# Attention and two feed-forward layers on one core: loading order and bias rows of the first heads

## The chip, the cores and the metric

The kernel runs on one core of a Trainium2 chip. The metric is the device time of one execution in microseconds, the median of the runs shown. All the work of the program, from the first load of its inputs to the last store of its output, lies in that time. TensorE is called PE below, VectorE DVE, ScalarE ACT, GpSimd POOL and SyncE SP, as the profile names them; SP issues nearly all DMAs, in order, on one queue.

## What is computed

The reference has three stages. The first is causal attention over 4 batches of 8 heads, 576 positions and a head dimension of 64, with a bias that comes from a running sum over the positions:

```
scores = scale * q @ k.T
cum    = cumsum(max(s, 0))                      # s: one number per position
scores = where(causal, -1e9, scores + min(-(cum[i] - cum[j]), 0))
attn   = softmax(scores);  x = attn @ v         # heads side by side: 2304 x 512
h = x @ w_in;  g = softplus(h);  x = g @ w_out                  # d_ff 2048
h = x @ w2_in; g = P(h) / (Q(h) + 1e-6);  out = g @ w2_out      # cubic over quadratic
```

The weights of both feed-forward layers arrive as 64-bit words, which the kernel turns into two 32-bit parts (high and low) on DVE, ACT and POOL.

## The kernel before

The kernel is recorded in an order of its own and then planned: `Planner` (L187) takes every recorded instruction as a `Step` with a modelled length (L109), walks through them engine by engine, and returns one order for each engine, which is kept up to a modelled time `UNTIL` (L70). A transfer's modelled length is its bytes over `DMA_RATE` plus `DMA_LATENCY` (L71). `queue_behind` (L445) ties newly recorded instructions behind the last one of their engine, so that the planner cannot put them in front of it. What has no such tie and no missing operand may be put anywhere.

Attention begins with "first" parts: the first 256 positions of the 16 heads of batches 0 and 1, handled as 8 pairs of heads. For pair i, `load_pair` (L507) loads q and k of two heads, 64 rows of 1024 numbers, into a tile `raw2` of 66 used rows. Rows 64 and 65 of that tile carry the running sum, so that one matmul of 66 rows gives score and bias together (L619). These two rows are called bias rows here. For pair 0 they are made in place: `load_s00` loads the two rows of s (tile `s00`), and `make_cum0` (L458) runs a scaling, a scan over both heads' 512 numbers and two scaled copies, one on ACT (L464) and one on DVE (L465). A zero in the tile `one` (L470) restarts the scan at the second head. For the other pairs the same is done once, on 16 rows for all eight pairs (`load_s0`, tile `s0_t`), into the tile `cumc`, and `load_cum` (L512) sends each pair's two rows from `cumc` to `raw2` by DMA.

`keep_order` (L437) fixes each engine's order in that preamble as it is written:

```
load_s00(); load_pair(0); load_s0()
for i in range(1, 4): load_pair(i)
load_v0(); make_cums()
for i in range(1, 4): load_cum(i)
```

Each head then goes through scores on PE (L619), masking with a row minimum (DVE, L595), exp (ACT, L612), the reciprocal of the sum (DVE, L613 and L614), a scaling (POOL, L615), three transposes (PE, L694), an evacuation (ACT, L673) and two matmuls with v (PE, L788). Tile `v2` holds v of four pairs. The results are split into high and low parts and feed the first layer (L1093 to L1095, then L1129 to L1131). Weight words come through `load_w` (L886) into tiles `raw64` and are turned in `conv_t` (L901; L908 to L910) and `conv_hl` (L913). The low parts are also stored to DRAM (L924) and read back as `w1l` (L934). The small vector `ab` of the second layer's coefficients is loaded into the tile `prm` and prepared by L1573 to L1576, which are recorded in the first layer.

At most eight transfers of SP are open at a time: transfer n waits until transfer n-8 has landed.

Of the kernel before, what the change touches and what calls it, by code (L numbers as in the profile page):

```python
# [8 lines left out]
F32 = mybir.dt.float32  # L9
F32R = mybir.dt.float32r  # L10
I32 = mybir.dt.int32
AF = mybir.ActivationFunctionType
# [55 lines left out]
          ("wide", "two"): 0.2, ("wide", "one"): 0.05, ("thin", "two"): 0.6, ("thin", "one"): 0.3}  # L68
HOLD, ROUNDS = 0.0, 6
UNTIL = 936.0  # L70
DMA_RATE, DMA_LATENCY, LANES = 320e3, 1.9, 8  # L71


class Access:
# [34 lines left out]
class Step:  # L109


    def __init__(self, i, tied):
        self.i, self.tied = i, tied
        self.engine = str(i.engine).split(".")[-1]
        acc = [[Access(x) for x in xs if getattr(getattr(x, "bass_ap", None), "tensor", None) is not None]
               for xs in (i.outs, i.ins)]
        self.outs, self.ins = acc
        self.dma, self.port = 0, None
        n = self.outs[0].elements if self.outs else 1
        psum = any(x.psum for x in self.outs + self.ins)  # L120
        wide = len(self.ins) > 1 and self.ins[1].dims[1][1] > 1
        if "DMA" in i.opcode:
            self.dma = 4 * n * self.outs[0].dims[0][1]
            self.busy = self.done = ISSUE.get(self.engine, 0.5)
        elif self.engine == "PE":
            turn = self.ins[0].tile.startswith("ident")
            full = not turn and "32r" not in str(i.ins[0].bass_ap.dtype)
            self.busy = 0.00085 * n if turn else 0.024 + 0.00162 * n if full else 0.012 + 0.000428 * n
            self.done = self.busy + 0.165
        elif self.engine == "Activation":  # L130
            more = max(0, len(self.outs) + len(self.ins) - 2)
            near = any(x.psum for x in self.ins)
            self.busy = (0.12 + 0.00079 * n + 0.07 * more) if near else (0.165 + 0.0008 * n + 0.095 * more)
            self.done = self.busy + 0.08
        elif self.engine == "DVE" and n == 1:
            self.busy, self.done = 0.115, 0.155
        elif self.engine == "DVE":
            one = len(self.ins) < 2 and not psum and i.opcode != "TensorCopy"
            self.busy = 0.06 + 0.00064 * n if one else 0.107 + 0.00105 * n
            self.done = self.busy + 0.06  # L140
            self.port = None if psum else "one" if one else "two"
        elif self.engine == "Pool":
            self.busy = 0.22 + 0.00205 * n if wide else 0.28 + 0.0007 * n
            self.done = self.busy + 0.03
# [42 lines left out]
class Planner:  # L187
# [27 lines left out]
    def forward(self, rank):  # L215
# [34 lines left out]
        for _ in range(n):  # L250
            best = None
            for e in self.engines:
                can = [(max(t, clock[e]), rank[k], k) for k in wait[e] for t in (earliest(k),) if t is not None]
                if can:
                    t0 = min(can)[0]
                    pick = min((c for c in can if c[0] <= t0 + HOLD), key=lambda c: (c[1], c[0], c[2]))
                    if best is None or pick[0] < best[0]:
                        best = pick
            t, _, k = best
            s = steps[k]  # L260
            wait[s.engine].remove(k)
            for x in tiles[k]:
                if x not in held:
                    tag = pool[x][0]
                    slots[tag].sort(key=lambda q: q[0])
                    self.slot_of[x] = slots[tag].pop(0)[1]
                    held.add(x)
                    last[tag] = max(last[tag], t)
                    while head[tag] < len(queue[tag]) and queue[tag][head[tag]] in held:
                        head[tag] += 1  # L270
            busy, done = s.busy, s.done
            if s.port:
                other = "Pool" if s.engine == "DVE" else "DVE"
                slow = SHARED.get((s.port, port[other]), 0.0) * max(0.0, min(clock[other] - t, busy))
                busy, done = busy + slow, done + slow
            port[s.engine] = s.port
            self.start[k], clock[s.engine] = t, t + busy
            self.end[k] = t + busy
            if s.dma:
                dma = max(dma, clock[s.engine]) + s.dma / DMA_RATE  # L280
                self.after[k] = dma + DMA_LATENCY - self.end[k]
                landed.append(dma + DMA_LATENCY)
            else:
                self.after[k] = done - busy
            done = self.end[k] + self.after[k]
# [54 lines left out]
def moe_chain_kernel(ctx, tc, qk0, v0, qk, vv, s0, s, w1, w2, ab, out):  # L340
    nc = tc.nc
# [9 lines left out]
    def t_w(name, shape, dt):  # L351
        return sb.tile(shape, dt, tag="W", bufs=NF, name=name)
# [99 lines left out]
        nc.sync.dma_start(out=cum_t["s00"][64:66], in_=s0[0:2])  # L452

    def load_s0():
        cum_t["s0"] = sb.tile([16, 2 * M + 4], F32, tag="tmp", bufs=1, name="s0_t")
        nc.sync.dma_start(out=cum_t["s0"], in_=s0)

    def make_cum0(st, one, t, to):  # L458
        n = 2 * M
        cst = st[:, n:n + 4]  # L460
        nc.vector.tensor_scalar(st[:, 0:n], st[:, 0:n], 0.0, 8.0, op0=ALU.max, op1=ALU.mult)
        nc.vector.tensor_tensor_scan(t, one, st[:, 0:n], 0.0, op0=ALU.mult, op1=ALU.add)
        t = t.rearrange("p (j s) -> p j s", j=2)
        nc.scalar.activation(to[:, :, 0], t, AF.Identity, scale=cst[:, 0:1], bias=cst[:, 1:2])  # L464
        nc.vector.tensor_scalar(to[:, :, 1], t, cst[:, 2:3], cst[:, 3:4], op0=ALU.mult, op1=ALU.add)  # L465

    def make_cums():
        one = t_w("one", [128, 2 * M], F32)
        nc.vector.memset(one, 1.0)
        nc.vector.memset(one[:, M:M + 1], 0.0)  # L470
        t = t_w("cum0", [128, 2 * M], F32)
        make_cum0(cum_t["s00"][64:66], one[64:66], t[64:66], raw2[0][64:66])
        cum_t["c"] = t_w("cumc", [16, 2, 2, M], F32)
        make_cum0(cum_t["s0"], one[0:16], t[0:16], cum_t["c"])

    def load_s():
        st = t_w("s_t", [128, S + 6], F32)
# [28 lines left out]

    def load_pair(i):  # L507
        t = t_q("raw2", [128, 2, 2, M], F32)
        nc.sync.dma_start(out=t[0:64], in_=qk0[i])
        raw2[i] = t  # L510

    def load_cum(i):  # L512
        nc.sync.dma_start(out=raw2[i][64:66], in_=cum_t["c"][2 * i:2 * i + 2])

    def load_v0():
        load_v2(0)
# [365 lines left out]
    xs_t = {}  # L882
    h_t, g_t, acc_t = {}, {}, {}
    raw64 = {}

    def load_w(m, ff, half, al=None):  # L886
        n = c2.index((ff, half)) if m else 0
        if n % 2:
            if "x" not in raw64:
                raw64["x"] = t_x("raw64x", [128, 2, 512, 2], I32)  # L890
            r = raw64["x"][:, n // 2 % 2]
        else:
            r = (al or t_r)("raw64", [128, 512, 2], I32)
        src = (w1, w2)[m][ff, :, half * 512:(half + 1) * 512].bitcast(I32)
        nc.sync.dma_start(out=r.rearrange("p a b -> p (a b)"), in_=src)
        raw64[m, ff, half] = r

    def conv(m, ff, half, hi, lo):
# [502 lines left out]
    if True:  # L1401
# [1 line left out]
        load_s00()  # L1403
        load_pair(0)
        load_s0()
        for i in range(1, 4):
            load_pair(i)
        load_v0()
        make_cums()
        for i in range(1, 4):  # L1410
            load_cum(i)
        order = keep_order()
        make_identity(nc, ident)
        nc.gpsimd.memset(mask, 0.0)
# [105 lines left out]
        for i in range(NU):  # L1520
# [41 lines left out]
            if u is not None:  # L1562
# [7 lines left out]
                if t4 >= 34 and t4 % 2 == 0 and FS + (t4 - 34) // 2 < NF:  # L1570
                    reload2(FS + (t4 - 34) // 2)
                if ph == 0 and T == 3 and ff == 8:
                    nc.sync.dma_start(out=abt, in_=ab)  # L1573
                    nc.vector.memset(qc, QC)
                    nc.vector.tensor_scalar(nega, abt[:, 0:4], -1.0, None, op0=ALU.mult)
                    nc.scalar.activation(babs, abt[:, 4:6], AF.Abs)  # L1576
                if ph == 0 and T == 5 and ff == 8:
                    load_y(0)
                if ph == 1:
# [102 lines left out]
```

## Time and profile before

| | us |
|---|---|
| median of 3 runs (lowest, highest) | 1022.59 (1021.87, 1023.67) |
| the profiled execution | 1024.62 |
| its span, first to last instruction | 1022.7 |
| PE busy | 998.6 (98%) |
| DVE busy | 789.9 (77%) |
| ACT busy | 763.7 (75%) |
| POOL busy | 469.1 (46%) |

Times in the profile count from the span's start. A row of the timeline is a run of like instructions on one engine; in brackets stands how long the engine was idle before it and what ended that. A wait is put down to the one that came last by the profile. A plain 32-bit matmul is counted as two instructions on PE, so that x4 in a row of L619 is the scores of one head. PEclk is the clock that the throttle granted to PE, as a share of full speed; a matmul's own duration tells beside it at which of its two levels (1.2 and 2.4 GHz) the array ran.

### The profile page before, as it was taken

The numbers are of one execution on the slowest core, as the hardware profiler recorded it, in microseconds if no ns is written. First come the engines' busy times: TensorE is split into PE (matmuls) and PEld (weight loads), VectorE is DVE, ScalarE is ACT, GpSimd is POOL, SyncE is SP. The second block draws the span as 40 slices with busy tenths as digits, with TensorE's granted clock in tenths as the row PEclk, the third lists the DMA queues.
The fourth block names the chain that finished last, engine by engine and source line by source line (L and its number), as shares of the span: only waits on it lengthen the run. The fifth ranks groups of instructions, "written<-read, shape, count | busy, mean of one in ns | idle before, by whom it ended". The sixth has DMA issues, their size and how long they took to land.

```text
span 1022.7 us, 18157 instructions
## 1 busy us (share of the span) xinstructions
PE 998.6 (98%) x5924; PEld 904.1 (88%) x5924; DVE 789.9 (77%) x1783; ACT 763.7 (75%) x1556; POOL 469.1 (46%) x464
## 2 busy tenths in 40 slices
PE   6989999999999999999999999999999999999998
PEld 5789999988999888899999999888888898889897
DVE  5799887877886887887677658887788778777765
ACT  5998777776885776776566667788779878788775
POOL 2776664411221112221446665676466457555542
PEclk9999999999999999999999999999999999999999
DMA  9778565474554654335999998628456656655300
GB/s 254 294 235 289 188 207 182 157 225 150 166 173 149 198 161 125 116 108 175 357 350 328 303 334 295 207 83 285 158 165 196 213 168 195 209 161 168 124 1 31
DMA packets 101069, 201.62 MB, mean 197 GB/s; under 512 B 11248, under 2 KB 30512, under 8 KB 100976
## 3 DMA queue, kind: packets, MB, share of 16 engines
q1 hardware_dynamic: 98432, 196.31, 58.6%
q10 hardware_dynamic: 2544, 4.16, 1.6%
q8 instruction: 47, 0.77, 0.3%
q14 instruction: 46, 0.38, 0.1%
HBM read 161.16 MB, written 35.19 MB: 192 GB/s over the span
## 4 chain that ended last, share of the span: by engine, by line
PE 87%; DVE 4%; DMA 3%; ACT 2%; POOL 2%; issue 1%; SPq 0%; POOLq 0%; DVEq 0%; ACTq 0%
PE h L1094 6%; PE at L1340 6%; PE h L1093 6%; PE h L1095 6%; PE at L763 5%; PE acc L1131 5%; PE acc L1130 5%; PE acc L1129 5%; PE h L1340 5%; PE acc L1270 4%; PE acc L1269 4%; PE acc L1271 4%; PE at L622 2%; PE at L623 2%; PE acc L1136 2%; PE acc L1137 2%
## 5 line engine op out<-in xcount | busy, mean ns | idle before, releaser
L615 POOL TENSOR_SCALAR PA<-PA,stat 128x384 f32<-128x384 f32 (+3 forms) x112 | 69.9, 629 | 179.7 <-DVE stat L614 113.4
L1093 PE MATMUL h<-xs,w1h 128*128 128x448 f32 (+1 forms) x360 | 122.9, 342 | 0.8 <-DVE stat L613 0.7
L1095 PE MATMUL h<-xs,w1l 128*128 128x448 f32 (+1 forms) x360 | 122.6, 342 | 0.9 <-DMA w1l<-l_d 0.8
L1094 PE MATMUL h<-xs,w1h 128*128 128x448 f32 (+1 forms) x360 | 122.6, 341 | 0.0
L1130 PE MATMUL acc<-gl,w1h 128*128 128x448 f32 (+1 forms) x352 | 119.3, 340 | 0.8 <-POOL gl L1397 0.8
L1131 PE MATMUL acc<-gh,w1l 128*128 128x448 f32 (+1 forms) x352 | 118.3, 339 | 0.3 <-POOL w1l L915 0.2
L1129 PE MATMUL acc<-gh,w1h 128*128 128x448 f32 (+1 forms) x352 | 118.4, 338 | 0.0
L1255 POOL TENSOR_TENSOR gl<-PA,gh 128x512 fp32r<-128x512 f32 x48 | 63.2, 1319 | 68.0 <-issue 51.7
L612 ACT ACTIVATE PA<-PA,stat 128x384 f32<-128x384 f32 (+3 forms) x112 | 63.9, 572 | 21.6 <-DVE stat L595 20.4
L1269 PE MATMUL acc<-w2b,gh 128*128 128x512 f32 x192 | 76.0, 396 | 0.0
L1270 PE MATMUL acc<-w2b,gh 128*128 128x512 f32 x192 | 75.8, 395 | 0.0
L1271 PE MATMUL acc<-w2b,gl 128*128 128x512 f32 x192 | 73.5, 394 | 0.0
L1093 PEld LDWEIGHTS h<-xs,w1h 128*128 128x128 f32 x360 | 68.0, 189 | 4.6 <-ACT pt L673 0.9
L1095 PEld LDWEIGHTS h<-xs,w1l 128*128 128x128 f32 x360 | 67.7, 188 | 4.8 <-DMA w1l<-l_d 1.0
L1094 PEld LDWEIGHTS h<-xs,w1h 128*128 128x128 f32 x360 | 67.9, 188 | 3.3
L1191 ACT ACTIVATE e<-h 128x448 f32<-128x448 f32 (+1 forms) x90 | 43.5, 483 | 36.2 <-PE h L1095 34.4
L1130 PEld LDWEIGHTS acc<-gl,w1h 128*128 128x128 f32 x352 | 66.2, 188 | 4.2 <-POOL gl L1397 1.0
L1131 PEld LDWEIGHTS acc<-gh,w1l 128*128 128x128 f32 x352 | 66.1, 188 | 3.6 <-POOL w1l L915 0.4
L1129 PEld LDWEIGHTS acc<-gh,w1h 128*128 128x128 f32 x352 | 66.2, 189 | 3.2
L1397 POOL TENSOR_TENSOR gl<-e,gh 128x256 fp32r<-128x256 f32 (+1 forms) x48 | 48.0, 1002 | 29.9 <-ACT gh L1395 21.0
L595 DVE CUSTOM_DVE_ANT_0 PA<-at,mask 128x384 f32<-128x384 f32 (+3 forms) x100 | 50.2, 519 | 7.4 <-PE at L623 5.0
L622 PE MATMUL at<-ht 128*128 128x512 f32 (+3 forms) x156 | 53.3, 347 | 0.1
(352 smaller groups left out, 3141.9 us busy)
## 6 DMA issues: line engine op xcount, KB each, us to landing
wa<-wa_d SPq DMA_DIRECT2D x100, 512.0 KB
w1l<-l_d SPq DMA_DIRECT2D x138, 256.0 KB
raw<-in_w_dram SPq DMA_DIRECT2D x48, 512.0 KB
raw<-in_qk_dram SPq DMA_DIRECT2D x24, 384.0 KB
l_d<-w1l SPq DMA_DIRECT2D x32, 256.0 KB
raw64x<-in_w_dram SPq DMA_DIRECT2D x16, 512.0 KB
wa_d<-pt SPq DMA_DIRECT2D x16, 512.0 KB
raw<-in_qk_dram SPq DMA_DIRECT2D x8, 576.0 KB
```

The lines of the kernel that those rows point to most:

```text
L615: nc.gpsimd.tensor_scalar(pt[:, 0:n], pt[:, 0:n], stat[:, i, 2:3], 1.0, op0=ALU.mult, op1=ALU.mult)
L622: nc.tensor.matmul(o, hq, p.ht[:, 1, k0:k0 + n], start=True, stop=False)
L1093: nc.tensor.matmul(h, wh[:, cs], xh, start=(k == 0), stop=False)
L1094: nc.tensor.matmul(h, wh[:, cs], xl, start=False, stop=False)
L1095: nc.tensor.matmul(h, wl[:, cs], xh, start=False, stop=(k == KD - 1))
L1129: nc.tensor.matmul(o, wh[:, cs], gh, start=first and not both, stop=False)
L1130: nc.tensor.matmul(o, wh[:, cs], gl, start=False, stop=False)
L1131: nc.tensor.matmul(o, wl[:, cs], gh, start=False, stop=last and (not both or m % 2 == 1))
L1269: nc.tensor.matmul(acc[m], gh[:, cs], wh, start=first, stop=False)
L1270: nc.tensor.matmul(acc[m], gh[:, cs], wl, start=False, stop=False)
L1271: nc.tensor.matmul(acc[m], gl[:, cs], wh, start=False, stop=last)
L1340: nc.tensor.matmul(o[:, p * 256:p * 256 + 256], x, z[:, k], start=first and p == k == n == 0, stop=(k, n) == (1, 2), skip_group_check=True)
```

## The change

The preamble is written in another order, and some tiles are laid out differently.

- Pair 0 is loaded in two transfers, one for each head (64 x 512 numbers each), and its bias rows are made head by head: a scaling, a scan and two copies of 256 numbers for head 0, then the same for head 1.
- The other pairs' bias rows are scanned with the heads on rows of their own: 48 rows of 256 numbers (rows 0 to 15 the first heads, 32 to 47 the second) in place of 16 rows of 512. The restart at column 256 falls away.
- v of batch 0 is loaded in two halves (pairs 0 and 1, pairs 2 and 3). The order on SP becomes pairs 0 and 1, half of v, pair 2, the bias rows of pairs 1 and 2, pair 3 and its rows, the rest of v.
- Each `load_w` is tied behind the one before it on SP, and the load of `ab` with its three small operations is tied behind what was recorded last on their engines.
- The planner's model changes: 400e3 in place of 320e3 for the transfer rate, twice the time for transfers of at most 64 rows, a length of its own for scans, and transfers that ACT issues no longer take SP's turn.

```
-DMA_RATE, DMA_LATENCY, LANES = 320e3, 1.9, 8
+DMA_RATE, DMA_LATENCY, LANES = 400e3, 1.9, 8
...
-            self.dma = 4 * n * self.outs[0].dims[0][1]
+            near = [x for x in self.outs + self.ins if x.pool]
+            rows = near[0].box[1] - near[0].box[0] if near else 128
+            self.dma = 4 * n * self.outs[0].dims[0][1] * (1 if rows > 64 else 2)
...
+        elif i.opcode == "TensorTensorScan" or "Scan" in i.opcode:
+            self.busy = 0.05 + 0.0023 * n
+            self.done = self.busy + 0.06
+            self.port = "two"
...
-            if s.dma:
+            if s.dma and s.engine != "SP":
+                self.after[k] = 2 * s.dma / DMA_RATE + DMA_LATENCY
+                dma += s.dma / DMA_RATE
+            elif s.dma:
...
     def load_s0():
-        cum_t["s0"] = sb.tile([16, 2 * M + 4], F32, tag="tmp", bufs=1, name="s0_t")
-        nc.sync.dma_start(out=cum_t["s0"], in_=s0)
+        cum_t["s0"] = sb.tile([48, M + 4], F32, tag="tmp", bufs=1, name="s0_t")
+        nc.sync.dma_start(out=cum_t["s0"], in_=s0[2:50, 0:M + 4])
...
     def make_cum0(st, one, t, to):
-        n = 2 * M
-        cst = st[:, n:n + 4]
-        nc.vector.tensor_scalar(st[:, 0:n], st[:, 0:n], 0.0, 8.0, op0=ALU.max, op1=ALU.mult)
-        nc.vector.tensor_tensor_scan(t, one, st[:, 0:n], 0.0, op0=ALU.mult, op1=ALU.add)
-        t = t.rearrange("p (j s) -> p j s", j=2)
-        nc.scalar.activation(to[:, :, 0], t, AF.Identity, scale=cst[:, 0:1], bias=cst[:, 1:2])
-        nc.vector.tensor_scalar(to[:, :, 1], t, cst[:, 2:3], cst[:, 3:4], op0=ALU.mult, op1=ALU.add)
+        nc.vector.tensor_scalar(st, st, 0.0, 8.0, op0=ALU.max, op1=ALU.mult)
+        nc.vector.tensor_tensor_scan(t, one, st, 0.0, op0=ALU.mult, op1=ALU.add)
+        for r, c, o in to:
+            nc.scalar.activation(o[:, 0], t[r], AF.Identity, scale=c[:, 0:1], bias=c[:, 1:2])
+            nc.vector.tensor_scalar(o[:, 1], t[r], c[:, 2:3], c[:, 3:4], op0=ALU.mult, op1=ALU.add)
...
+        st = cum_t["s00"][64:66]
+        for j in range(2):
+            m = slice(j * M, j * M + M)
+            make_cum0(st[:, m], one[64:66], t[64:66, m], [(slice(0, 2), st[:, 2 * M:2 * M + 4], raw2[0][64:66, j])])
         cum_t["c"] = t_w("cumc", [16, 2, 2, M], F32)
-        make_cum0(cum_t["s0"], one[0:16], t[0:16], cum_t["c"])
+        st = cum_t["s0"]
+        rows = slice(0, 16), slice(32, 48)
+        make_cum0(st[:, 0:M], one[0:48], t[0:48, 0:M], [(r, st[r, M:M + 4], cum_t["c"][:, j]) for j, r in enumerate(rows)])
...
     def load_pair(i):
         t = t_q("raw2", [128, 2, 2, M], F32)
-        nc.sync.dma_start(out=t[0:64], in_=qk0[i])
+        for j in ((0, 1), (1, 2)) if i == 0 else ((0, 2),):
+            nc.sync.dma_start(out=t[0:64, j[0]:j[1]], in_=qk0[i, :, j[0]:j[1]])
...
+        k0 = len(nc.cur_bb.bb.instructions)
         nc.sync.dma_start(out=r.rearrange("p a b -> p (a b)"), in_=src)
+        queue_behind(w_last, k0)
+        w_last.update({i.engine: i for i in traced(k0)})
...
         load_s0()
-        for i in range(1, 4):
-            load_pair(i)
-        load_v0()
+        load_pair(1)
+        load_v0(0, 2)
+        load_pair(2)
         make_cums()
-        for i in range(1, 4):
-            load_cum(i)
+        load_cum(1)
+        load_cum(2)
+        load_pair(3)
+        load_cum(3)
+        load_v0(2, 4)
...
                 if ph == 0 and T == 3 and ff == 8:
+                    last = {i.engine: i for i in traced()}
+                    k0 = len(nc.cur_bb.bb.instructions)
                     nc.sync.dma_start(out=abt, in_=ab)
...
+                    queue_behind(last, k0)
```

The order of SP's first transfers, before (the tiles `raw2_127`, `raw2_131`, `raw2_133`, `raw2_135` are pairs 0 to 3, `raw64` are weight words, `<-cumc` are bias rows):

```order
L452 DMA s00_125<-in_s0_dram 2x516
L509 DMA raw2_127<-in_qk0_dram 64x1024
L456 DMA s0_t_129<-in_s0_dram 16x516
L509 DMA raw2_131<-in_qk0_dram 64x1024
L509 DMA raw2_133<-in_qk0_dram 64x1024
L509 DMA raw2_135<-in_qk0_dram 64x1024
L520 DMA v2_137<-in_v0_dram 128x1536
L895 DMA raw64_1799<-in_w1_dram 128x1024
L895 DMA raw64_1937<-in_w1_dram 128x1024
L1573 DMA prm_123<-in_ab_dram 128x6
L513 DMA raw2_131<-cumc_147 2x1024
```

And in the changed kernel, where pairs 0 to 3 are `raw2_127`, `raw2_132`, `raw2_136` and `raw2_158`:

```order
L461 DMA s00_125<-in_s0_dram 2x516
L521 DMA raw2_127<-in_qk0_dram 64x512 x2
L465 DMA s0_t_130<-in_s0_dram 48x260
L521 DMA raw2_132<-in_qk0_dram 64x1024
L530 DMA v2_134<-in_v0_dram 128x768
L521 DMA raw2_136<-in_qk0_dram 64x1024
L525 DMA raw2_132<-cumc_149 2x1024
L525 DMA raw2_136<-cumc_149 2x1024
L521 DMA raw2_158<-in_qk0_dram 64x1024
L525 DMA raw2_158<-cumc_149 2x1024
L530 DMA v2_134<-in_v0_dram 128x768
L521 DMA raw2_328<-in_qk0_dram 64x1024
```

The bias rows of pair 1 move ahead of pair 3, half of v, two loads of weight words and the load of `ab`. The first weight words now come as the 15th and 16th transfer, and those two that stood 8th and 9th (the 23rd and 24th piece of the first layer's weights) stand behind the 22 pieces before them.

The order of PE from the third instruction on, before (`gh` are probabilities, `pt` their transposes):

```order
L619 MATMUL h_204<-raw2_127 128x128
L619 MATMUL h_204<-raw2_127 128x256
L694 MATMUL acc_218<-ident_122,gh_170 128x128 x3
L694 MATMUL h_241<-ident_122,gh_203 128x128 x3
L788 MATMUL acc_238<-pt_217,v2_137 128x256
L619 MATMUL at_225<-raw2_131 128x128
L619 MATMUL at_225<-raw2_131 128x256
```

And in the changed kernel:

```order
L633 MATMUL h_211<-raw2_127 128x128
L633 MATMUL h_211<-raw2_127 128x256
L708 MATMUL acc_225<-ident_122,gh_177 128x128 x3
L633 MATMUL at_232<-raw2_132 128x128
L633 MATMUL at_232<-raw2_132 128x256
L708 MATMUL h_248<-ident_122,gh_210 128x128
L802 MATMUL acc_245<-pt_224,v2_134 128x256
```

Pair 1's first scores stand behind the transposes of head 0 alone, ahead of those of head 1 and of head 0's product with v.

The order of DVE at its start, before:

```order
L465 TENSOR_SCALAR raw2_127<-cum0_142,s00_125 2x2x256
L461 TENSOR_SCALAR s0_t_129<-s0_t_129 16x512
L462 SCALAR_TENSOR_TENSOR cum0_142<-one_139,s0_t_129 16x512
L465 TENSOR_SCALAR cumc_147<-cum0_142,s0_t_129 16x2x256
L595 ISA gh_170,stat_169<-acc_171,mask_121 128x128
```

And in the changed kernel:

```order
L472 TENSOR_SCALAR raw2_127<-cum0_140,s00_125 2x256
L468 TENSOR_SCALAR s0_t_130<-s0_t_130 48x256
L469 SCALAR_TENSOR_TENSOR cum0_140<-one_138,s0_t_130 48x256
L472 TENSOR_SCALAR cumc_149<-cum0_140,s0_t_130 16x256 x2
L609 ISA gh_177,stat_176<-acc_178,mask_121 128x128
```

The first masking still stands behind the whole chain for the other pairs, whose operations are half as long.

## Rows read from the trace of the kernel before

**Rows 1.** Busy us of the engines, share of the span, instructions.

```profile
PE 998.6 (98%) x5924; PEld 904.1 (88%) x5924; DVE 789.9 (77%) x1783; ACT 763.7 (75%) x1556; POOL 469.1 (46%) x464
```

**Rows 2.** First 40 us: length; busy PE, PEld, DVE, ACT, POOL; PEclk; DMA; GB/s.

```profile
0.00:40.00 40.00, 30.36 (x145) 24.74 (x145) 26.74 (x119) 25.65 (x74) 19.96 (x38) 1.00 0.87 262
```

**Rows 3.** Timeline, PE: start, length, what, idle before it and its end.

```profile
4.93 1.62 PE L619 MATMUL acc<-raw 66*128 66x128 f32 x4 [4.93 <-DMA raw<-in_qk_dram]
...
6.34 1.49 PE L619 MATMUL h<-raw 66*128 66x128 f32 x4
...
9.87 0.90 PE L694 MATMUL acc<-ident,gh 128*128 128x128 f32 x3 [2.04 <-POOL gh L615]
...
13.66 1.65 PE L619 MATMUL at<-raw 66*128 66x128 f32 x4 [1.09 <-DMA raw<-cumc]
```

**Rows 4.** Chain that ended last, 7 to 24 us: start, length, work or transfer.

```profile
7.74 5.88 DMA raw<-cumc
...
19.57 0.64 PE at L694 x3
20.21 1.28 PE at L619 x4
...
21.92 1.22 PE h L788 x4
23.14 0.66 PE h L619 x4
```

**Rows 5.** Timeline, DVE and ACT at the start.

```profile
2.20 0.42 DVE L461 TENSOR_SCALAR s<-s 2x512 f32<-2x512 f32 x1 [0.68 <-DMA s<-in_s_dram]
...
2.66 1.22 DVE L462 TENSOR_TENSOR_SCAN cum<-one,s 2x512 f32<-2x512 f32 x1
...
5.20 0.42 DVE L461 TENSOR_SCALAR s_t<-s_t 16x512 f32<-16x512 f32 x1 [0.63 <-DMA s_t<-in_s_dram]
...
6.90 0.81 ACT L464 ACTIVATE cumc<-cum,s_t 16x512 f32<-16x512 f32 x1 [2.18 <-DVE cum L462]
6.90 0.53 DVE L465 TENSOR_SCALAR cumc<-cum,s_t 16x512 f32<-16x512 f32 x1
...
7.36 0.27 DVE L595 CUSTOM_DVE_ANT_0 gh<-acc,mask 128x128 f32<-128x128 f32 x1
```

**Rows 6.** Timeline, SP: the issue of two transfers.

```profile
0.74 0.37 SPq L452 DMA_DIRECT2D s<-in_s_dram  x1
...
1.78 0.58 SPq L456 DMA_DIRECT2D s_t<-in_s_dram  x1
```

**Rows 7.** Transfers issued in the first 40 us: count and size of each.

```profile
raw<-in_w_dram SPq DMA_DIRECT2D x12, 512.0 KB
raw<-in_qk_dram SPq DMA_DIRECT2D x8, 256.0 KB
v<-in_v_dram SPq DMA_DIRECT2D x2, 768.0 KB
```

**Rows 8.** Three stretches of 2 us, columns as in rows 2.

```profile
4.00:6.00 2.00, 1.07 (x4) 1.01 (x5) 1.30 (x3) 0.71 (x1) 0.00 (x0) 1.00 1.02 227
...
10.00:12.00 2.00, 2.00 (x8) 1.42 (x8) 0.00 (x0) 0.98 (x2) 1.84 (x5) 1.00 1.02 408
...
24.00:26.00 2.00, 1.75 (x12) 1.41 (x10) 1.78 (x7) 2.00 (x8) 0.44 (x1) 1.00 1.03 225
```

**Rows 9.** Timeline, ACT: the operations of a head.

```profile
7.67 0.40 ACT L612 ACTIVATE gh<-gh,stat 128x128 f32<-128x128 f32 x1
...
7.98 0.18 ACT L612 ACTIVATION_READ_ACCUMULATOR gh<-gh,stat 128x1 f32 x1
...
8.57 0.51 ACT L612 ACTIVATE gh<-gh,stat 128x256 f32<-128x256 f32 x1
...
10.80 0.49 ACT L673 ACTIVATE pt<-acc 128x384 f32<-128x384 f32 x1 [1.24 <-PE acc L694]
```

**Rows 10.** A stretch of 5 us, columns as in rows 2.

```profile
90.00:95.00 5.00, 5.00 (x41) 4.91 (x41) 4.96 (x14) 4.21 (x11) 2.83 (x3) 1.00 1.05 401
```

**Rows 11.** Timeline, PE: a wait for a transfer in the first layer.

```profile
76.20 0.38 PE L1095 MATMUL h<-xs,w1l 128*128 128x256 f32 x1 [0.76 <-DMA w1l<-l_d]
```

More of the change, by code (lines that the diff above doesn't have):

```diff
@@ L454, in load_s0 @@
     def load_s0():
-        cum_t["s0"] = sb.tile([16, 2 * M + 4], F32, tag="tmp", bufs=1, name="s0_t")
-        nc.sync.dma_start(out=cum_t["s0"], in_=s0)
+        cum_t["s0"] = sb.tile([48, M + 4], F32, tag="tmp", bufs=1, name="s0_t")
+        nc.sync.dma_start(out=cum_t["s0"], in_=s0[2:50, 0:M + 4])
     def make_cum0(st, one, t, to):
-        n = 2 * M
-        cst = st[:, n:n + 4]
-        nc.vector.tensor_scalar(st[:, 0:n], st[:, 0:n], 0.0, 8.0, op0=ALU.max, op1=ALU.mult)
-        nc.vector.tensor_tensor_scan(t, one, st[:, 0:n], 0.0, op0=ALU.mult, op1=ALU.add)
-        t = t.rearrange("p (j s) -> p j s", j=2)
-        nc.scalar.activation(to[:, :, 0], t, AF.Identity, scale=cst[:, 0:1], bias=cst[:, 1:2])
-        nc.vector.tensor_scalar(to[:, :, 1], t, cst[:, 2:3], cst[:, 3:4], op0=ALU.mult, op1=ALU.add)
+        nc.vector.tensor_scalar(st, st, 0.0, 8.0, op0=ALU.max, op1=ALU.mult)
[3 more added lines that the diff above has]
+            nc.vector.tensor_scalar(o[:, 1], t[r], c[:, 2:3], c[:, 3:4], op0=ALU.mult, op1=ALU.add)
     def make_cums():
-        one = t_w("one", [128, 2 * M], F32)
+        one = t_w("one", [128, M], F32)
         nc.vector.memset(one, 1.0)
-        nc.vector.memset(one[:, M:M + 1], 0.0)
         t = t_w("cum0", [128, 2 * M], F32)
-        make_cum0(cum_t["s00"][64:66], one[64:66], t[64:66], raw2[0][64:66])
+        st = cum_t["s00"][64:66]
+        for j in range(2):
+            m = slice(j * M, j * M + M)
+            make_cum0(st[:, m], one[64:66], t[64:66, m], [(slice(0, 2), st[:, 2 * M:2 * M + 4], raw2[0][64:66, j])])
         cum_t["c"] = t_w("cumc", [16, 2, 2, M], F32)
-        make_cum0(cum_t["s0"], one[0:16], t[0:16], cum_t["c"])
+        st = cum_t["s0"]
+        rows = slice(0, 16), slice(32, 48)
+        make_cum0(st[:, 0:M], one[0:48], t[0:48, 0:M], [(r, st[r, M:M + 4], cum_t["c"][:, j]) for j, r in enumerate(rows)])
     def load_s():
@@ L508, in load_pair, with load_cum, load_v0 @@
         t = t_q("raw2", [128, 2, 2, M], F32)
-        nc.sync.dma_start(out=t[0:64], in_=qk0[i])
+        for j in ((0, 1), (1, 2)) if i == 0 else ((0, 2),):
+            nc.sync.dma_start(out=t[0:64, j[0]:j[1]], in_=qk0[i, :, j[0]:j[1]])
         raw2[i] = t
[L512 to L516, printed above, removed]
+    def load_cum(i, queue=nc.sync):
+        queue.dma_start(out=raw2[i][64:66], in_=cum_t["c"][2 * i:2 * i + 2])
+    def load_v0(i, n):
+        if i == 0:
+            v2[0] = t_x("v2", [128, 4, 2, 3, D], F32)
+        nc.sync.dma_start(out=v2[0][:, i:n], in_=v0[0, :, i:n])
     def load_v2(b):
@@ L884, in moe_chain_kernel @@
     raw64 = {}
+    w_last = {}
     def load_w(m, ff, half, al=None):
@@ L1650 @@
     cs0 = _np.array([[0, 1, 1, 0], [-1, 0, 0, 1]], _np.float32)
+    se = _np.repeat(inputs["s"][0:2, :, 0:256].reshape(8, 2, 1, 256), 2, axis=2)
+    s0 = _np.zeros((50, 516), se.dtype)
+    s0[0:2, 0:512], s0[0:2, 512:516] = se[0].transpose(1, 0, 2).reshape(2, 512), cs0
+    for j in range(2):
+        r = slice(2 + 32 * j, 18 + 32 * j)
+        s0[r, 0:256], s0[r, 256:260] = se[:, j].reshape(16, 256), _np.tile(cs0, (8, 1))
     vp = _np.zeros((B, H, 640, D), v.dtype)
@@ L1659 @@
         "vv": c(vp.reshape(B, H // 2, 2, 5, 128, D).transpose(0, 1, 4, 3, 2, 5)),
-        "s0": c(_np.concatenate([_np.repeat(inputs["s"][0:2, :, 0:256].reshape(8, 512), 2, axis=0), _np.tile(cs0, (H, 1))], axis=1)),
+        "s0": s0,
         "s": c(_np.concatenate(
```

## The prediction

> **What bounds the kernel now.** I read the busy times first. PE works for 998.6 of 1022.7 us [rows 1], so 24.1 us are all that PE is idle. Of these 9.64 lie in the first 40 us, where PE is busy for 30.36 [rows 2]. A change of the preamble can win there and hardly anywhere else: behind it PE is nearly full, and time won early is kept.
>
> Next I read PE's timeline from the start [rows 3]. Its first matmul starts at 4.93, when pair 0's transfer has landed. The scores of heads 0 and 1 end at 6.34 + 1.49 = 7.83. Then PE is idle for 2.04 us until the probabilities of head 0 are there (9.87), and for 1.09 us more until 13.66, when the bias rows of pair 1 land. Idle until 13.66: 4.93 + 2.04 + 1.09 = 8.06 us. Behind 13.66 PE has no idle time in the timeline before 24 us.
>
> The chain that ended last says why pair 1 comes so late [rows 4]: it goes through one transfer of two bias rows, 5.88 us from 7.74 to 13.62. The transfer is 8 KB, so this is the time behind the transfers ahead of it. They are pair 0 and three more pairs (4 x 256 KB), v (768 KB) and two loads of weight words (2 x 512 KB) [rows 7], with the two small loads of s some 2850 KB. They move at 227 GB/s while pairs of 64 rows flow and at 408 GB/s while v and weights do [rows 8].
>
> The chain shows a second thing. The scores of one head take 1.28 us at 20.21 and 0.66 us at 23.14 [rows 4], with the granted clock at 1.00 in all these stretches [rows 8]. So the array ran at 1.2 GHz until about 23 us and at 2.4 GHz after, and it rose after PE had worked without idle time from 13.66, for 9.3 us.
>
> **The change, part by part.** *Pair 0 by head.* The s rows of pair 0 land at 2.20 as before. The scaling is then 0.42 us and the scan 1.22 [rows 5], and ACT's copy is 0.81 as in the like operation on `cumc` [rows 5]. With 256 numbers in place of 512 I take half of each plus a little for the fixed part: 0.24 + 0.67 + 0.42 and gaps, so head 0's rows stand at about 3.6. The load of q and k then decides. Its first half is 128 KB less, 0.58 us at 227 GB/s [rows 8]. Head 0's scores start at 4.93 - 0.6 = 4.3. Bounds: 4.93 (the landing does not depend on size) and 3.6 (the rows decide).
>
> *The other pairs' rows.* Their s load is issued one issue of 0.58 us later [rows 6], behind the same bytes of pair 0. It landed at 5.20; I take 5.4, the bounds are 5.2 and 5.8. From there 0.24 + 0.67 and, on DVE, two copies of half of 0.53 (0.28 each): DVE is through at about 6.9 in place of 6.90 + 0.53 = 7.43 [rows 5]. DVE's first masking, at 7.36 before, stands right behind this chain in both orders, so head 0's softmax starts some 0.5 us earlier, and its transposes at 9.3 in place of 9.87. PE's idle time up to there is then 4.3 at the start, plus 9.3 less the end of the four scores (4.3 + 2.9 = 7.2), so 2.1: together 6.4 us.
>
> *Rows sent ahead.* Ahead of pair 1's rows there now stand 3 x 256 + 384 KB, some 1200 KB with the loads of s. At 227 and 408 GB/s that is 3.5 + 1.0 us from about 2.4 on, so the queue is through at about 7. The rows are issued at about 7.2, when ACT has made its second copy (6.3 + 2 x 0.42). A transfer with nothing ahead of it took 2.20 - 0.74 = 1.46 us [rows 5, 6], one in the full queue 5.88. Landing lies between 8.7 and 13.1. I take 9.2, near the first, since the queue is nearly empty by then. PE reaches these scores at 9.3 + 0.9 = 10.2 (behind the transposes of head 0), so anything up to 10.2 costs nothing, and the wait of 1.09 us goes.
>
> *What PE gains.* From 13.66 on PE is the bound for the next ten microseconds, so I count its idle time: 8.06 - 6.4 = 1.66 us less. That is work at 1.2 GHz, worth 0.83 us at full speed. The scores at 10.2 in place of 13.66 look like 3.5 us, but in the kernel before PE had by 13.66 also transposed head 1 and begun head 0's product with v; this work now stands behind. *The clock.* If the array needs the same 9.3 us of unbroken work, it rises at 9.3 + 9.3 = 18.6 in place of 23.0. For 4.4 us PE runs at twice the speed, 2.2 us of full-speed work more. ACT caps this. A head costs PE 0.64 + 1.28 + 1.22 = 3.14 us at the low level [rows 4], so 1.57 at the high one; it costs ACT 0.40 + 0.18 + 0.51 + 0.18 + 0.49 = 1.76 us [rows 9]. In 4.4 us ACT passes 2.5 heads where slow PE passed 1.4; 1.1 heads more are 1.1 x 1.57 = 1.7 us. ACT is full from 24 us on (2.00 of 2.00 [rows 8]), so the early start is worth this much there also.
>
> The Trainium skill, "TensorE: Matmul & The Clock Gate", Part 1, says that the array's clock follows how busy PE has lately been, and that the point of the rise varies between runs of the same kernel. By the first half the 1.7 us would stand; by the second they would be anything between none and all of it. The rows show one rise in one execution and cannot tell.
>
> *What costs nothing.* One more issue on SP (0.58 us [rows 6]) lies before SP has anything to wait for. The memset and the scaling on DVE get shorter. The load of `ab` and its three small operations leave the start, where DVE and ACT waited for other things, and now stand in the first layer far ahead of their first use in the second. If the load were late there, DVE would wait in front of its operation for the length of a transfer. *The weight words* that stood 8th and 9th are 1024 KB less in the first 14 us, and come at about 90 us instead. PE is busy there for 5.00 of 5.00 us [rows 10]; I take nothing, with 0 and 2.6 us (1024 KB at 401 GB/s) as ends. *The new plan* of the remaining order I take at zero, with 1.5 us to either side: 24.1 - 9.64 = 14.5 us of idle time is all that it can shrink or must not double.
>
> Sum: 0.8 + 1.7 = 2.5 us. The profiled execution took 1024.62 us and would take 1022.1. The median of the runs, 1022.59, is 2.0 us below that execution, so the predicted median is 1020.1.
>
> **The rivals.** *The clock rises when it did.* If 23 us is set by something that does not move (the phase, or the mix of matmuls), only the idle time counts: 0.8 us, 1021.8. For it: the rise came not after the first unbroken work (4.93 to 7.83) but much later. Against: nothing in the kernel happens at 23 us. *The clock rises soon after 13.* The transposes and products with 128 rows now stand earlier between the 66-row scores. From 14 to 23 us ACT then passes 5.1 heads in place of slow PE's 2.9, and 2.2 x 1.57 = 3.5; with the 0.8 this is 4.3 us, 1018.3.
>
> *Slower: the postponed weight words.* Two loads, 1024 KB, enter the stretch around 90 us, where the DMA engines are at 1.05 of their time and 401 GB/s [rows 10]. They hold up everything on SP's queue by 2.6 us: the parts of later heads and the stores of low words. PE has already waited 0.76 us for such a low part at 76.20 [rows 11]. If all of it reaches PE, it takes back the 2.5, and where the clock does not help either, 2.6 - 0.8 makes the kernel 1.8 us slower, 1024.4. It decides from the point at which PE's waits between 85 and 110 us grow by more than 0.8 us. Against it: DVE and PE have work of several heads open there, and the 22 pieces before them come with 1024 KB less ahead of them.
>
> *The change does not reach its target.* The s load of the other pairs lands a microsecond later than I take it, because it is issued later and stands behind two transfers. DVE's first masking waits for it; head 0's softmax then starts when it did, the idle time moves from 13 us to 9 us, and the time is 1022.6.
>
> **How the numbers follow.** The forecast gets 0.44, the clock that stays 0.22, the early clock 0.18, the postponed words 0.08, no effect 0.08. The range reaches from the early clock with 0.9 us of a better plan, 1017.4, to the forecast's loss of all its terms and 0.6 us of a worse plan, 1023.2. What is left out is most of the postponed words and the better half of the early clock's plans, under 2 in 10. A measurement of this kernel can tell about 0.2%, 2.0 us, from no change. Faster by more than that: four fifths of the forecast, the early clock and a little of the first rival, 0.56. Slower by more: the postponed words, 0.08. Within: 0.36.
>
> **What would show it.** In the changed kernel's profile: PE's first matmul near 4.3; head 0's transposes near 9.3; pair 1's scores near 10.2 with no wait for a transfer of bias rows in front of them; scores of 0.66 us from about 18.6 on; PE's idle time in the first 40 us below 8.2. The forecast is wrong if pair 1's scores wait for their rows beyond 11, if scores still take 1.28 us at 22, or if PE's idle time between 40 and 140 us grows by more than a microsecond.

## The result and the profile after

The changed kernel takes 1028.92 us (median of 6 runs, 1028.19 to 1031.61) against 1022.57 (1021.37 to 1023.67): ratio 1.0069, 95% interval 1.0055 to 1.0083. It is 6.4 us slower where 2.5 us of gain were forecast. PE's busy time fell a little from [rows 1]:

```profile
PE 995.4 (97%) x5924; PEld 904.8 (88%) x5924; DVE 788.8 (77%) x1786; ACT 764.7 (74%) x1558; POOL 472.0 (46%) x464
```

The work is the same, then, and the loss is nearly all waiting: of a span of 1026.9 us PE is idle for 31.5, before for 24.1 of 1022.7. The timeline of PE at the start (start, length, what, idle before it and its end) answers to [rows 3]:

```profile
4.27 1.62 PE L633 MATMUL acc<-raw 66*128 66x128 f32 x4 [4.27 <-DMA raw<-in_qk_dram]
...
9.46 0.90 PE L708 MATMUL acc<-ident,gh 128*128 128x128 f32 x3 [2.30 <-POOL gh L629]
10.16 1.49 PE L633 MATMUL at<-raw 66*128 66x128 f32 x4
...
17.93 0.87 PE L633 MATMUL at<-raw 66*128 66x128 f32 x4
...
29.52 0.55 PE L708 MATMUL acc<-ident,gh 128*128 128x128 f32 x3 [1.79 <-POOL gh L629]
```

The preamble does what was forecast: first scores at 4.27, transposes at 9.46, pair 1's scores at 10.16 with no wait for bias rows, and scores at the high clock from 17.93 on (0.87 in place of 1.49). Then a wait of 1.79 us appears at 29.52. The first 40 us, columns as in [rows 2], end with no more work done than before (30.16 against 30.36):

```profile
0.00:40.00 40.00, 30.16 (x160) 25.74 (x161) 28.11 (x123) 27.96 (x83) 21.10 (x39) 1.00 0.84 237
```

In front of that wait, DVE's timeline shows the scaling of the running sum for the rest of attention. Its load is issued at 15.08, behind v of the second batch, and DVE, working in its planned order, waits for it:

```profile
26.72 0.46 DVE L506 TENSOR_SCALAR s_t<-s_t 128x576 f32<-128x576 f32 x1 [1.22 <-DMA s_t<-in_s_dram]
```

That fits a lead that is lost, not 6 us, and e5 below takes this wait away and wins nothing by it. PE waits once more for what is made of these sums, 1.52 us at 54.75, and behind that it runs at the low level for some 3.5 us (0.41 for a matmul that takes 0.28 from 59 us on):

```profile
54.75 0.47 PE L637 MATMUL at<-st 68*128 68x512 f32 x1 [1.52 <-DMA st<-cum_d]
...
57.45 0.41 PE L1148 MATMUL acc<-gl,w1h 128*128 128x256 f32 x1
...
60.24 0.28 PE L1148 MATMUL acc<-gl,w1h 128*128 128x256 f32 x1
```

The greater loss comes later. At 336 us (the first results of the first layer's third group of tokens) the changed kernel is still 2.1 us ahead (337.9 before, 335.8 after), at 637 it is 4.7 behind (632.9 and 637.6). The windows between, of the kernel before (columns as in [rows 2]):

```profile
500.00:520.00 20.00, 20.00 (x99) 18.38 (x99) 12.63 (x19) 12.05 (x23) 9.27 (x7) 1.00 1.02 371
520.00:540.00 20.00, 20.00 (x100) 18.38 (x99) 16.08 (x28) 13.57 (x26) 9.27 (x7) 1.00 0.97 337
540.00:560.00 20.00, 20.00 (x100) 18.38 (x99) 16.42 (x21) 12.00 (x22) 12.17 (x10) 1.00 0.97 324
560.00:580.00 20.00, 20.00 (x100) 18.43 (x99) 11.50 (x18) 12.58 (x25) 12.67 (x11) 1.00 0.93 299
```

And of the changed kernel:

```profile
500.00:520.00 20.00, 20.00 (x101) 18.56 (x100) 13.64 (x20) 12.99 (x24) 10.05 (x8) 1.00 1.03 368
520.00:540.00 20.00, 19.66 (x98) 17.92 (x97) 13.44 (x24) 11.75 (x23) 7.88 (x6) 1.00 1.02 358
540.00:560.00 20.00, 18.12 (x88) 15.81 (x86) 12.14 (x20) 12.63 (x25) 10.06 (x8) 1.00 1.04 375
560.00:580.00 20.00, 16.33 (x72) 15.02 (x73) 14.39 (x19) 11.42 (x21) 14.28 (x12) 0.83 0.93 323
```

PE was full here and now loses 0.34 + 1.88 + 3.67 us, and in the last window its clock is down to 0.83. The DMA engines are full (1.02 to 1.04) until 560 us, where they had a little room. What was added stands in the transfers issued from 480 to 560 us: the stores of converted second-layer weights (`wa_d`), before and after.

```profile
wa_d<-w2a SPq DMA_DIRECT2D x7, 256.0 KB
wa_d<-PA SPq DMA_DIRECT2D x2, 256.0 KB
```

```profile
wa_d<-w2a SPq DMA_DIRECT2D x16, 256.0 KB
wa_d<-PA SPq DMA_DIRECT2D x3, 256.0 KB
```

Ten more stores, 2.5 MB, are planned into these 80 us. The timelines of SP, POOL, DVE, ACT and PE there, in that order:

```profile
553.42 0.37 SPq L1032 DMA_DIRECT2D wa_d<-PA  x1
...
552.44 1.15 POOL L1415 TENSOR_TENSOR gl<-e,gh 128x448 fp32r<-128x448 f32 x1
559.47 1.26 POOL L933 TENSOR_TENSOR PA<-tc,PA 128x512 fp32r<-128x512 f32 x1 [5.87 <-DMA wa_d<-PA]
...
560.76 1.33 DVE L926 TENSOR_SCALAR tc<-raw 128x512 int32<-128x512 int32 x1 [2.32 <-POOL PA L933]
562.36 0.68 DVE L928 SCALAR_TENSOR_TENSOR tc<-raw,tc 128x512 int32<-128x512 int32 x1
...
554.12 0.53 ACT L1079 ACTIVATE yt<-yt 128x384 fp32r<-128x384 f32 x1 [4.18 <-DMA yt<-y_d]
...
563.07 0.54 ACT L1183 ACTIVATE yb<-acc 128x448 f32<-128x448 f32 x1 [3.49 <-DVE tc L928]
...
558.09 0.36 PE L1111 MATMUL h<-xs,w1h 128*128 128x448 f32 x1
563.67 0.74 PE L1147 MATMUL acc<-gh,w1h 128*128 128x448 f32 x1 [5.21 <-ACT yb L1183]
...
567.19 0.55 PE L1112 MATMUL h<-xs,w1h 128*128 128x448 f32 x1
567.56 0.37 PE L1113 MATMUL h<-xs,w1l 128*128 128x448 f32 x1
```

Read from the bottom, each wait names the next. PE waits for a PSUM bank that ACT has to copy out (`yb`). The copy waits for a buffer whose weight words DVE is still converting (`tc`). DVE waits for POOL to free a `tc` buffer. POOL stands for 5.87 us until a store out of one of the three `PA` buffers has landed; the only such store issued before 557 is that of 553.42, so it took some 6.05 us. ACT meanwhile has waited 4.18 us for a load of y's rows. Both were transfers behind the same queue. After its 5.21 us of idle time PE runs ten matmuls in 3.89 us (563.67 to 567.56); at the later spacing of 0.20 they take about 2.05. Together 5.21 + 1.84 = 7.05 us, about the swing from 2.1 ahead to 4.7 behind (6.8).

### The profile page after: what moved, and what is told of

Same layout as the page of the kernel before. It is cut to its first block, busy times and chain, and to the rows that moved or that the text cites. A ratio compares the mean times of both kernels' runs of the same rounds, so it can differ in the third digit from the quotient of the medians.

```text
span 1026.9 us, 18187 instructions
## 1 busy us (share of the span) xinstructions
PE 995.4 (97%) x5924; PEld 904.8 (88%) x5924; DVE 788.8 (77%) x1786; ACT 764.7 (74%) x1558; POOL 472.0 (46%) x464
## 5 line engine op out<-in xcount | busy, mean ns | idle before, releaser
L933 POOL TENSOR_TENSOR w1l<-tc,w1h 128x512 fp32r<-128x512 f32 x32 | 46.3, 1451 | 19.3 <-PE acc L1149 7.1
```

## Experiments

Each ratio is to the kernel before, run beside it.

### Only the planner's new costs undone (e1)

```
-DMA_RATE, DMA_LATENCY, LANES = 400e3, 1.9, 8
+DMA_RATE, DMA_LATENCY, LANES = 320e3, 1.9, 8
...
+            self.dma = 4 * n * self.outs[0].dims[0][1]
...
-        elif i.opcode == "TensorTensorScan" or "Scan" in i.opcode:
...
-            if s.dma and s.engine != "SP":
...
+            if s.dma:
```

> The changed kernel with the planner's model as before (rate 320e3, no doubling for transfers of up to 64 rows, scans and ACT's transfers as before): new preamble and ties alone. Theory: the start is kept (first matmul 4.3, pair 1's scores 10.2), no wait of PE above 2 us between 540 and 600, 1020 to 1023. Rival (ties of the weight words): a wait of PE for an evacuation of 3 us or more stays, 1026 or more. Rival (any new plan scatters by several us): the time may lie anywhere from 1018 to 1030, with waits at other places.

Measured: 1019.91 us, ratio 0.9968 (0.9954 to 0.9981): faster than both kernels. PE works for 32.29 us of the first 40, and is full from 540 to 580. The new preamble and the ties therefore do no harm; the new costs cost some 9 us in this pair of orders.

### The preamble alone (e7)

The four costs as in e1, and both ties (of `load_w` and of `ab`) taken out as well.

> The kernel before with the new preamble alone: old model, no tie of the weight words or of ab. Theory: start as in the changed kernel, no long wait of PE, 1019.5 to 1022. Rival (the lead of the start cannot be kept, since loads or DVE, ACT and POOL bind between 20 and 60 us): the lead of 3 us at 20 us is gone by 60 us, 1022 to 1023.5.

Measured: 1023.46 us, ratio 0.9998 (0.9986 to 1.0009): no gain, as the rival had it. Here the planner put head 0's product with v ahead of pair 1's scores, which start at 12.43 in place of 10.16, so the start is not quite that of the changed kernel. It looked as if the ties gained 3 us; e4, e10 and e11 below took this up.

### The split of y's rows moved behind the evacuations (e3)

The order is the changed kernel's own; only two operations on ACT and two on DVE move: `hold` puts the first split of y's rows behind the next two `yb` copies of its engine.

```
+def hold(p, line):
...
     _, lines, start = best
+    lines = {e: hold(p, line) for e, line in lines.items()}
```

> The order of the changed kernel with one thing moved: the first two splits of the second layer's input (ACT L1079, DVE L1080) stand behind the two evacuations of the first layer's fifth tile that follow them, in place of ahead of them. Theory (the plan believes transfers land too early, so ACT stands 4.2 us at 549.9 waiting for y, and PE then 5.2 us for an evacuation): PE's 5.2 us wait falls below 1.5 us, the half-speed stretch at 563 to 567 is gone, and the time falls by 5 to 7 us, to 1022 to 1024. Rival (the evacuation waits for its buffer, which weight words hold because their loads are tied to one order): PE's wait stays above 3.5 us and the time within 2 us of 1028.9.

Measured: 1028.22 us, ratio 1.0046 (1.0033 to 1.0060). ACT's wait for y's load is gone, and PE still waits 5.4 us for `yb`. In POOL's timeline the same wait stands as in the changed kernel:

```profile
559.38 1.26 POOL L950 TENSOR_TENSOR PA<-tc,PA 128x512 fp32r<-128x512 f32 x1 [5.56 <-DMA wa_d<-PA]
```

So the load of y was a second victim and not the cause. I had taken ACT's in-order wait for the cause; that theory fell here. The rival put the wait down to the ties of the weight words; e4 below has no such tie, and PE still waits 4.3 us for `yb`.

### The load of s ahead as well (e5)

e3, and on SP the load `s_t` right behind the first two loads of weight words.

> As the kernel with the late splits, and besides the load of all heads' s (SP L489, 291 KB) is issued right behind the first two loads of weight words, ahead of pair 5's load and the second batch's v. Theory: DVE's wait of 1.22 us at 26.7 for this load goes, PE's wait of 1.79 us at 27.7 falls below 0.6, and the time is 1 to 2 us below that with late splits alone. Rival (DVE, ACT and POOL are full there anyway): the wait moves to another engine and the time differs by less than 0.7 us.

Measured: 1027.53 us, ratio 1.0039 (1.0024 to 1.0054). DVE's wait for `s_t` is gone, but the scaling starts no earlier, at 27.21: DVE now waits 1.28 us for scores from PE ahead of it, and PE, which no longer waits at 29.5, waits 2.63 us for ACT at 22.41. The wait moved to another engine, as the rival had it, and nothing is gained beside e3. PE's wait for `yb` stays at 5.2 us.

### Same order, half of the stored bytes (e9)

This puts the remaining theory to the test: the plan counts on 400 GB/s, and the queue may not carry them. The 27 stores of 256 KB are halved, the twelve of 512 KB are not.

```
-            nc.sync.dma_start(out=row_a(ff)[:, :, h], in_=f(t).rearrange("p (b c) -> p b c", b=2))
+            nc.sync.dma_start(out=row_a(ff)[:, 0:1, h], in_=f(t).rearrange("p (b c) -> p b c", b=2)[:, 0:1])
...
+            self.dma *= 2 if n == 256 and self.outs[0].tile.startswith("wa_d") else 1
```

The last line keeps the planner's cost, and with it every engine's order: in the two traces all engines run the same operations in the same order. The readers take the stored half twice.

> The changed kernel in its own order on every engine, but each store of a converted block of output weights that goes by itself (27 of 256 KB in the stretch from 480 to 560 us) writes only its first half, and its readers take that half twice, so the values of the second half are left out of the result. If the loss at 563 us comes from the DMA queue, whose plan counts on 400 GB/s and which was full from 500 to 560 us (shares of 1.02 to 1.04), then with 3.5 MB less the DMA share there falls to 0.92 or less, POOL's wait of 5.9 us for a store falls under 2, PE's wait of 5.2 us for yb under 1.5, and the time to 1021.5 to 1024. If the order itself stalls (ACT waits for y's load or for a conversion that stands too early in its line, whatever the queue carries), PE's wait stays at 4 to 5.5 us and the time at 1026.5 to 1029.

Measured: 1021.79 us, ratio 0.9988 (0.9974 to 1.0001), 7 us less than the changed kernel in the same order. The 540 to 580 us windows, POOL and PE:

```profile
540.00:560.00 20.00, 18.46 (x91) 16.80 (x91) 15.51 (x21) 13.60 (x26) 12.08 (x9) 1.00 1.00 356
560.00:580.00 20.00, 20.00 (x100) 18.58 (x100) 14.29 (x19) 12.64 (x24) 15.48 (x12) 1.00 0.96 308
...
553.69 1.48 POOL L934 TENSOR_TENSOR PA<-tc,PA 128x512 fp32r<-128x512 f32 x1 [1.43 <-DMA wa_d<-PA]
...
558.32 0.47 PE L1148 MATMUL acc<-gh,w1h 128*128 128x448 f32 x1 [1.54 <-ACT yb L1184]
```

POOL's wait falls from 5.87 to 1.43, PE's from 5.21 to 1.54 (just over the 1.5 expected), and the clock stays at 1.00 in these windows. One expectation missed: the DMA share did not fall to 0.92. It is still 1.00 in 540 to 560. As the order is the same, the same transfers can be compared. One of the first of these stores leaves SP at 488.88 in the changed kernel and at 488.85 here, later ones at 507.21 and 506.11, 546.10 and 541.94, and the store out of `PA` for which POOL waits at 553.42 and here at

```profile
548.46 0.32 SPq L1033 DMA_DIRECT2D wa_d<-PA  x1
```

So in the changed kernel the queue falls some 5 us further behind over these 65 us. In e9 the work behind moves up by as much and fills it. The store is not much faster when half as long: POOL goes on 5.23 us after its issue, against 6.05. It is issued 4.96 us earlier, and most of what POOL gains comes from that. It is the lateness that costs, not the full queue.

### The rate alone, both ways (e6, e8)

e6 is the changed kernel with 320e3 and its other three new costs; e8 has 400e3 and the other three undone.

> The changed kernel with the planner's DMA rate back at 320e3, its other three new costs (doubled time of loads of 64 rows or fewer, the scan, ACT's transfers) kept. If the rate is what costs the time: 1018.5 to 1022, DMA share in 540 to 560 us at 0.93 to 0.98, no wait of PE of over 2.5 us behind 100 us. If the other costs do, or if any new cost scatters the plan: 1025 to 1029.

> The changed kernel with the planner's rate of 400e3 and the other three new costs undone. If the rate is what costs the time: 1026 to 1030, with a DMA share of 1.02 or more from 500 to 560 us and a wait of PE of 3 us or more near 560. If the other three costs do: 1018.5 to 1022.

Measured: e6 1022.24 us, ratio 0.9983 (0.9974 to 0.9993); e8 1033.68, ratio 1.0098 (1.0083 to 1.0113). e6 has no wait for `yb`, six stores `wa_d<-w2a` from 480 to 560 us, and this window:

```profile
540.00:560.00 20.00, 20.00 (x101) 18.56 (x100) 13.28 (x19) 12.03 (x23) 9.91 (x8) 1.00 0.91 307
```

e8 has sixteen such stores again, and on PE:

```profile
567.91 0.74 PE L1138 MATMUL acc<-gh,w1h 128*128 128x448 f32 x1 [5.38 <-ACT yb L1174]
```

e6 lies just above the range expected of it (1018.5 to 1022), e8 3.7 us above its own (1026 to 1030). The rate is the cause of the loss near 560 us: with it alone the loss is there, and without it alone it is gone. The other three costs bring nothing without the rate (0.9983 against 0.9968, intervals that overlap). That e8 is some 3 us slower than the changed kernel (1.0098 against 1.0069) does not show that they help: the two lose the same near 560 us ("One stretch in every run" below) and differ ahead of it, where orders scatter by as much.

### Other rates (e12, e13)

e1 with 360e3 and with 280e3.

> The kernel of e1 with the planner's DMA rate at 360e3, about what the queue carried from 500 to 520 us when it was full (359 to 372 GB/s). If the loss grows with the rate as the backlog does: 1022 to 1028, DMA share of 500 to 560 us between those of 320e3 and 400e3 and a wait for yb of 1 to 4 us. If there is a step once the plan's rate goes over what the queue carries: 1019 to 1022, with no wait for yb of over 1.5 us.

> The kernel of e1 with the planner's DMA rate at 280e3, under what the queue carries. If only a plan that counts on too much is harmful: 1018.5 to 1022, as e1, with no wait for yb of over 1.5 us and the differences those of a new order. If the plan must be near the true rate: over 1023, with transfers issued later and PE waiting for them somewhere behind 100 us.

| rate in the plan (old costs, new preamble) | us | ratio (95%) |
|---|---|---|
| 280e3 (e13) | 1026.83 | 1.0029 (1.0018 to 1.0041) |
| 320e3 (e1) | 1019.91 | 0.9968 (0.9954 to 0.9981) |
| 360e3 (e12) | 1022.38 | 0.9985 (0.9974 to 0.9996) |
| 400e3 (e8) | 1033.68 | 1.0098 (1.0083 to 1.0113) |

e12 shows what a full queue costs. Its windows:

```profile
500.00:520.00 20.00, 20.00 (x101) 18.57 (x100) 12.43 (x20) 12.14 (x23) 9.32 (x7) 1.00 1.05 387
520.00:540.00 20.00, 20.00 (x101) 18.56 (x100) 16.05 (x25) 13.01 (x25) 9.21 (x7) 1.00 1.05 379
540.00:560.00 20.00, 20.00 (x101) 18.57 (x100) 15.88 (x23) 12.17 (x24) 11.96 (x9) 1.00 1.03 383
```

The queue is fuller than in the changed kernel, with 14 of these stores, and PE never waits there: 379 to 387 GB/s were carried and 360 were counted on. So the loss does not grow in step with the rate; it fits these runs that it comes when the plan promises more than is carried. Four rates in one kernel do not show where the step lies. The 280e3 run was expected at e1's level and is 0.6% slower by the ratios, twice the 3 us by which orders at 320e3 differ: counting on too little harmed as well, in this one order. Its loss is spread (PE 34.13 us busy from 60 to 100 us, against 36.70 in e1, and a wait of 1.7 us behind `yb`); which late transfers make it was not followed up.

### The ties (e4, e10, e11)

e4 is the changed kernel without the tie of `load_w`; e10 and e11 are e1 without the one tie or the other.

> The changed kernel without the tie that keeps the loads of weight words in the order of the program. If the ties are what made the old planner's run with them 3.5 us faster than the preamble alone (1019.9 against 1023.5), the time rises by 2 to 4 us, to 1031 to 1033. If that difference was the scatter of a new order, it may go either way, within 1025 to 1031, and the wait of PE near 563 us stays as long as the rate is 400e3.

> The kernel with the old planner's costs and the new preamble (1019.9 us in e1), without the tie of the weight words' loads. If this tie is worth the 2.4 us that it was worth under the new costs (1031.3 against 1028.9): 1021.5 to 1023.5, the level of the preamble alone. If not: 1019 to 1021.

> The same kernel with the tie of the weight words' loads, but without the tie that holds back the load of a and b and what is made of it. If the tie of the weight words is what gains: 1019 to 1021, as e1. If the other tie is: 1022 to 1024, as the preamble alone.

Measured: e4 1031.33 us, ratio 1.0079 (1.0061 to 1.0097), with a wait of 4.3 us for `yb`, not distinct from the changed kernel's 1.0069. e10 1020.52, ratio 0.9966 (0.9954 to 0.9978); e11 1020.65, ratio 0.9969 (0.9958 to 0.9980). Neither tie is worth anything by itself. Why the kernel without both is 3 us slower than those with one stays open: the two together, or the accident of one order among these.

### One stretch in every run

Two copies on ACT bracket the stretch from 472 to 633 us, here before and in the changed kernel:

```profile
471.91 0.55 ACT L1165 ACTIVATE yb<-acc 128x448 f32<-128x448 f32 x1
632.87 0.53 ACT L1165 ACTIVATE yb<-at 128x448 f32<-128x448 f32 x1
```

```profile
469.99 0.55 ACT L1183 ACTIVATE yb<-acc 128x448 f32<-128x448 f32 x1
637.64 0.54 ACT L1183 ACTIVATE yb<-at 128x448 f32<-128x448 f32 x1
```

From the one to the other, in the profiled execution of each kernel:

| rate in the plan | us |
|---|---|
| 400e3 | 167.7 (changed), 167.1 (e3), 166.6 (e5), 165.1 (e4), 167.5 (e8) |
| 400e3, stores halved | 160.8 (e9) |
| 360e3 | 159.0 (e12) |
| 320e3 | 161.0 (before), 160.3 (e1), 160.3 (e6), 159.0 (e7), 159.0 (e10), 160.3 (e11) |
| 280e3 | 160.6 (e13) |

Five orders planned at 400e3 lose 4 to 7 us here, and eight planned lower, among them the kernel before, lose nothing. The scatter of orders does not explain that: among those eight the stretch differs by 2.0 us. It is not the whole of the distance: at the first copy e1 (466.01) is already 4 us ahead of the changed kernel. e6 (470.19), with 320e3 and the other new costs, is not, so these 4 us are not shown to come from the rate.

## Why the prediction was wrong

**The step that failed** is "*The new plan* of the remaining order I take at zero, with 1.5 us to either side". I saw the line that sets 400e3 and did not price it as a claim about the queue. The rows it read showed 227 GB/s for pairs of 64 rows and, in stretches of 2 and 5 us, 408 and 401 [rows 8, 10]; the windows of the kernel before would have shown 371 GB/s in a full stretch of 20 us, from 500 to 520, where loads and stores are mixed. The changed kernel carried 358 to 375 GB/s while full. Against 400 that is 33 GB/s short in the mean of its three windows, so of 60 us of transfers planned about 5 are late by the end; this is an estimate that takes the plan's queue as full throughout. The comparison with e9 bears it out: 4.96 us at the store that POOL waits for. Eight transfers may be open on SP, then everything behind them slips together, and engines that work in a planned order wait for what was planned to be there. The measured waits of 4.18 and 5.87 us are of that size. The bound "14.5 us of idle time is all that it can shrink or must not double" was right and far wider than the 1.5 us I gave.

The Trainium skill, "DMA: Bandwidth & Descriptors", section "Where 436 GB/s comes from", puts the HBM side's limit at about 358 GB/s for a core and says that it binds between HBM and SBUF, not the fabric's 435. By that rule a plan at 400 promises 12% too much. The trace does not bear 358 out as a limit: the full windows shown here carried 358 to 387 GB/s. But they lie below 400; that is the sentence I should have weighed against this change.

**What held.** *Pair 0 by head*: 4.3 forecast, 4.27 measured. *The other pairs' rows*: transposes at 9.3, measured 9.46. *Rows sent ahead*: pair 1's scores at 10.2 without a wait, measured 10.16. *The clock*: 18.6 forecast; scores take 1.49 us at 10.16 and 0.87 at 17.93, so the rise came a little earlier, and in this trace both rivals on it (unchanged at 23, soon after 13) are out. That is luck. e5 has the same PE order up to there and starts each group within 0.4 us of it. Its six scores from 12.9 on take 1.12 us where the changed kernel's take 1.92:

```profile
12.93 1.92 PE L633 MATMUL acc<-raw 66*128 66x128 f32 x6
```

```profile
12.91 1.12 PE L661 MATMUL acc<-raw 66*128 66x128 f32 x6
```

There the rise came soon after 13, and the clock fell again behind the wait of 2.63 us at 22.41. In e7 scores still take 1.49 at 22.18. So what the preamble does to the clock differs from order to order and from execution to execution, and no run isolates the 1.7 us of that term. "PE's idle time in the first 40 us below 8.2" failed in the changed kernel (9.84), because of the plan's waits between 20 and 40 us. Under the old costs it held in e1 (40 - 32.29 = 7.71) but not in e10 (8.34), e7 (8.78) or e11 (10.46), so it is no good sign of the time. One sign of a wrong forecast came true: PE's idle time between 40 and 140 us grew by 1.10 us (6.06 to 7.16), with the wait at 54.75. The sum for the preamble, 2.5 us or a ratio of 0.9976, lies among the kernels that have it under 320e3: 0.9966 to 0.9998. These differ by 3 us with the order alone, so the runs cannot say how much of e1's gain is the preamble's.

**The rivals.** *The postponed weight words* was the only slower one, at 1024.4. It had the right kind of cause, traffic moved into a full stretch, but the wrong place: PE's waits grew at 563 us, and between 85 and 110 us they did not (1.63 us before, 1.53 after). *The change does not reach its target* is refuted by the timeline of the start. None of the four let the planner's costs move transfers hundreds of microseconds from the edit, though that is where they act.

## What to carry to other kernels

A constant in a planner is a statement about the hardware: before pricing an edit to it, look for the windows in which that resource is full and compare what they carry with the constant. Where the constant lay above, here, in-order engines stalled where the plan was densest, half a millisecond from the rest of the edit; of the four values tried here, 320 and 360 did no harm where 358 to 387 were carried, and 280 lost again. When PE's wait names an engine, follow the names until one ends at a DMA, and test that DMA by shrinking its bytes with the order kept.

The version to keep is e1 (or e10, e11): the new preamble with the old costs, 0.9968 (0.9954 to 0.9981) of the kernel before.

## What was not expected of the hardware

- A 256 KB store issued into the full queue took some 6.05 us (553.42 to 559.47), where the plan's two figures, 400 GB/s and 1.9 us, give 2.6 with nothing ahead of it.
- PE's idle time of 5.21 us was followed by 3.89 us of matmuls at 0.55 to 0.74 us in place of 0.37. After 1.54 us of it in e9, with PE full before, the granted clock of the window stayed at 1.00; after 1.52 us at 54.75 in the changed kernel, with other waits before, the clock fell too. The length of the wait alone does not tell. The Trainium skill, "TensorE: Matmul & The Clock Gate", Part 1, says that the clock follows how busy PE has lately been; the trace agrees. The long wait cost a third more than its own length (1.84 us beside 5.21).
- Halving 27 stores did not empty the queue. The work behind moved up and kept it at 1.00 of its time.
- The clock's first rise differed by 5 us between two kernels whose PE does the same until then: about 13 us in e5, about 18 in the changed kernel.
